# Token blocks of 512 in place of 448, 128 rows in a product of 113, and a subtraction moved to the head of its step: agent attention with two expert layers on one core

## The chip, the core and the metric

The kernel runs on one core of one Trainium2 chip. The core's engines run beside each other, each in the order of its own queue, and wait for each other by semaphores: TensorE (PE, matrix products and transposes into PSUM), VectorE (DVE), ScalarE (ACT), GpSimd (POOL, here only constants and some loads) and SyncE (SP, which issues DMAs). Before a matmul its stationary operand, the weights, is loaded by an instruction of its own (PEld in the profile); the other operand moves through the array column by column. The metric is device time in microseconds (us), the median of several executions; lower is better.

## What is computed

12480 tokens of 128 channels go through an attention with 49 agents and then two layers of width 2048 with squared ReLU, all in float32:

```python
def sm(a, b):                                   # softmax of scaled scores
    s = scale * (a @ b.transpose(0, 2, 1))
    e = np.exp(s - s.max(-1, keepdims=True))
    return e / (e.sum(-1, keepdims=True) + 1e-09)
agent_v = sm(agents, k) @ v
x = sm(q, agents) @ agent_v                     # 12480 x 128
g = s * np.maximum(x @ w_in, 0)**2 + b          # first layer
x = g @ w_out
h = np.maximum(x @ w_in2, 0)                    # second layer
out = (h * h) @ w_out2
```

## The kernel before

**Numbers in two parts.** Nearly all products run on numbers of 32 bits that TensorE takes rounded. To keep precision each operand is split into a high part (rounded) and a low part (the rest): `split` casts and then subtracts. A product of two such operands is three matmuls: low weights by high data, high by low, high by high.

**Preparation.** The attention of the agents over the keys gives a 49 x 128 matrix (`av`). `m_piece` multiplies it with `w_in`, so that the first layer's up product can go straight from the query softmax: `M`, high and low, holds `agent_v @ w_in` on partitions 0 to 48 and again on 64 to 112. The softmax of a block's queries stands in `X` with its high part in one of these places and its low part in the other, the gap between being zero. One product over 113 partitions (`KS` = 64 + 49) then sums both parts. Weights are decoded into their two parts on DVE and ACT by `fill`, in small steps that go on into the first 22 steps of the main loop.

**The main loop.** `blocks` cuts the tokens into 27 blocks of 448 (4 x 112) and one of 384. Each block takes 8 steps (`NPR`), and a step handles 2 of the 16 chunks of the width 2048. In a step PE does, in this order: `up1` of block t (four matmuls, 113 rows, low and high part of M), one query task of block t+1, `up2` of an earlier block (six), and the two `down` products of earlier steps (six each). Layer 2 runs 11 steps behind layer 1, and a down product 2 steps behind its up product. After an up product ACT applies ReLU and square, and DVE casts (`gh`) and subtracts (`gl`).

**Query tasks of block t+1 during block t.** Loading: two or three blocks ahead, on SP. `q_transpose` casts the high part `qh` (ACT, last step of the block before). `q_low` subtracts the low part `ql` (DVE) in step 0, behind `up1`'s cast and subtraction in DVE's queue. Step 1: `q_scores_T`, two matmuls with the stacked agents `aS` as weights (line 213). Step 2: `q_back`, a pair of transposes (line 228). Then softmax on ACT and DVE, and in step 6 `q_stack`, another pair of transposes (line 259), from which `X` of the next block is written.

The order of all engines is that of the code; nothing reorders it. The queue of each engine is filled step by step as the loop writes it. Line 594 is `up1`'s matmul, 604 `up2`'s, 620 both downs', 213 the score matmuls', 186 `q_low`'s subtraction, 124 and 125 the cast and subtraction of `split`.

Of the kernel before, what the change touches and what calls it, by code (L numbers as in the profile page):

```python
# [9 lines left out]
F32 = mybir.dt.float32  # L10
F32R = mybir.dt.float32r
# [3 lines left out]
ALU = mybir.AluOpType  # L15
AX = mybir.AxisListType

P = 128
BP = 112
SQ = 32  # L20
LAG = 2
WC = 512
# [11 lines left out]
DIRECT = 3  # L34
# [11 lines left out]
def tile_agent_attention_two_moe(  # L46
# [14 lines left out]
    nc = tc.nc  # L61
    _, N, C = q.shape
    NA = agents.shape[1]
# [7 lines left out]
    def cut(rows, most=P):  # L71

        pieces, t = [], 0
        while N - t >= rows * most:
            pieces.append((t, most, rows))
            t += rows * most
        if t < N:
            left = N - t
            p = next(x for x in range(min(most, left), 0, -1) if left % x == 0 and left // x <= rows)
            pieces.append((t, p, left // p))  # L80
        return pieces

    blocks = cut(4, BP)
    kblocks = cut(8)
    NT = sum(j for _, _, j in kblocks)

# [19 lines left out]
    aT = const.tile([P, GAP], F32, name="aT")  # L106
    s_sb = const.tile([P, 1], F32, name="s_sb")
    M = [const.tile([P, DFF], F32R, name=f"M{x}") for x in "hl"]
    av = [const.tile([P, KS], F32R, name=f"av{x}") for x in "hl"]
    b_sb = const.tile([P, 1], F32, name="b_sb")  # L110
    ones_r = const.tile([P, P], F32R, name="ones_r")
    y1_bias = const.tile([P, 1], F32, name="y1_bias")
    wo = [const.tile([P, NCH, C], F32R, name=f"wo{x}") for x in "hl"]
    wi2 = [const.tile([P, DFF], F32R, name=f"wi2{x}") for x in "hl"]
    wo2 = [const.tile([P, NCH, C], F32R, name=f"wo2{x}") for x in "hl"]
    stacks = [const.tile([P, 4, GAP], F32, name=f"stack{i}") for i in range(2)]
    sTs = [const.tile([KS, 256], F32, name=f"sT{i}") for i in range(2)]
    aS = const.tile([P, KS], F32R, name="aS")
    halves = (0, slice(0, NA)), (1, slice(GAP, KS))
    Xs = [const.tile([KS, 512], F32R, name=f"X{i}") for i in range(2)]  # L120

    def split(dst, src, eng_lo, copy=nc.vector.tensor_copy):

        copy(dst[0], src)  # L124
        eng_lo.tensor_tensor(out=dst[1], in0=src, in1=dst[0].bitcast(F32), op=ALU.subtract)  # L125
# [80 lines left out]
    def q_scores_T(t):  # L206

        _, p, j = blocks[t]
        n = p * j
        x = qT.pop(t)  # L210
        ps = small("ps_sT")
        for z in (1, 0):
            nc.tensor.matmul(out=ps[:KS, :n], lhsT=aS, rhs=x[z][:, :n], start=(z == 1), stop=(z == 0))  # L213
        sT = sTs[t % 2]
        for h, to in halves:
            nc.scalar.copy(sT[to, :2 * p], ps[:NA, 2 * p * h:2 * p * (h + 1)])
        for h, to in halves:
            nc.vector.tensor_tensor(
                out=sT[to, :2 * p], in0=ps[GAP:KS, 2 * p * h:2 * p * (h + 1)], in1=sT[to, :2 * p], op=ALU.add
            )  # L220
        q_sT[t] = sT
# [157 lines left out]
    def m_piece(i):  # L379

        sl = slice(i * WC, (i + 1) * WC)
        ps = small("ps_M")
        for z, (x, w) in enumerate(((av[0], wi[1]), (av[1], wi[0]), (av[0], wi[0]))):
            nc.tensor.matmul(out=ps[:KS], lhsT=x, rhs=w[:, sl], start=(z == 0), stop=(z == 2))
        split((M[0][:KS, sl], M[1][:KS, sl]), ps[:KS], nc.vector, nc.scalar.copy)

    with tc.manual_schedule():

        with tc.tile_pool(name="pre", bufs=1) as pre, tc.tile_pool(name="kp", bufs=2) as kp:
# [43 lines left out]
            nc.tensor.transpose(out=ps[:, :NA], in_=ag, identity=ident[:NA, :NA])  # L433
            nc.vector.tensor_copy(aT[:, :NA], ps[:, :NA])
            nc.vector.tensor_copy(aS[:, :NA], aT[:, :NA])
            nc.vector.tensor_tensor(out=aS[:, GAP:], in0=aT[:, :NA], in1=aS[:, :NA].bitcast(F32), op=ALU.subtract)
            mxa = pre.tile([P, 8, NA], F32, name="mxa")

            def k_transpose(g):
# [148 lines left out]
        def up1(t, i):  # L588
            n = blocks[t][1] * blocks[t][2]
            ps = ps_h.tile([P, 2, 512], F32, tag="h", name="ps_h1")  # L590
            for c in range(2):
                sl = slice((2 * i + c) * P, (2 * i + c + 1) * P)
                for z in (1, 0):
                    nc.tensor.matmul(out=ps[:, c, :n], lhsT=M[z][:KS, sl], rhs=X[t], start=(z == 1), stop=(z == 0))  # L594
            G1[t, i] = hidden(ps, n, 1, nc.scalar.copy if t * NPR + i in HI_ACT else nc.vector.tensor_copy)

        def up2(t, i):
# [48 lines left out]
        for st in range(total + L2 + LAG + 1):  # L646
# [10 lines left out]
                m_piece(2 + M_AT.index(st))  # L657
            if st < len(FILL_L):
                fill(FILL_L[st])
            if t < NB:  # L660
                up1(t, i)
                if i == 0:
                    for u, far in ((t + 2, t + 2 < DIRECT), (t + 3, DIRECT <= t + 3 < NB)):
                        if far:
                            q_load(u)
                if t + 1 < NB:
                    if t + 2 < NB and i == NPR - 2:
                        q_turn(t + 2)
                    elif t + 2 < NB and i == NPR - 1:
                        q_transpose(t + 2)  # L670
                    elif i == 0 and t + 1 >= DIRECT:
                        q_low(t + 1)
                    if i == QS[0]:
                        (q_scores if t + 1 < DIRECT else q_scores_T)(t + 1)
                    elif i == QS[1] and t + 1 >= DIRECT:
                        q_back(t + 1)
                    elif i == QS[3]:
                        q_norm(t + 1)
                    elif i == QS[4]:
                        q_stack(t + 1)  # L680
# [43 lines left out]
```

## Time and profile before

| | us |
|---|---|
| median of 3 runs | 1110.24 (1109.37 to 1111.34) |
| profiled execution, its own time | 1110.83 |
| its span, first to last instruction | 1108.9 |
| PE busy | 1092.6 |
| weight loads busy | 1009.6 |
| DVE busy | 954.7 |
| ACT busy | 952.8 |
| mean granted TensorE clock | 0.993 |

Busy times overlap. The end of a matmul is modelled and matmuls are pipelined: a 448-column matmul shows 0.36 us while the next one starts 0.20 us after it. So a matmul's cost is read from the starts. In the rows below a line of the timeline gives start (us), duration (us), engine, line, operation, output <- operands, shapes; text in brackets is the time the engine sat idle before it and what ended that.

### The profile page before, as it was taken

The numbers are of one execution on the slowest core, as the hardware profiler recorded it, in microseconds if no ns is written. First come the engines' busy times: TensorE is split into PE (matmuls) and PEld (weight loads), VectorE is DVE, ScalarE is ACT, GpSimd is POOL, SyncE is SP. The second block draws the span as 40 slices with busy tenths as digits, with TensorE's granted clock in tenths as the row PEclk, the third lists the DMA queues.
The fourth block names the chain that finished last, engine by engine and source line by source line (L and its number), as shares of the span: only waits on it lengthen the run. The fifth ranks groups of instructions, "written<-read, shape, count | busy, mean of one in ns | idle before, by whom it ended". The sixth has DMA issues, their size and how long they took to land.

```text
span 1108.9 us, 15258 instructions
## 1 busy us (share of the span) xinstructions
PE 1092.6 (99%) x5651; PEld 1009.6 (91%) x5651; DVE 954.7 (86%) x1413; ACT 952.8 (86%) x1201; POOL 12.5 (1%) x36
## 2 busy tenths in 40 slices
PE   9988999999999999999999999999999999999998
PEld 8877899999999999999999999999999999999997
DVE  6898888888888888888888888888888888888876
ACT  6658988988898889888888888888888888889876
POOL 2100000000000000000000000000000000000000
PEclk9898999999999999999999999999999999999999
DMA  9999939964999909999099991899963999700001
GB/s 343 291 162 15 8 11 10 14 19 12 15 8 15 21 9 8 15 15 19 5 15 15 15 8 17 13 15 7 15 19 12 9 14 15 12 9 1 9 9 16
DMA packets 1163202, 34.95 MB, mean 32 GB/s; under 512 B 1145575, under 2 KB 1159544, under 8 KB 1163128
## 3 DMA queue, kind: packets, MB, share of 16 engines
q1 hardware_dynamic: 1160224, 27.57, 103.5%
q0 software_dynamic: 1728, 6.29, 1.9%
q8 instruction: 44, 0.72, 0.4%
q14 instruction: 30, 0.25, 0.1%
q10 hardware_dynamic: 1176, 0.12, 0.1%
HBM read 27.58 MB, written 6.39 MB: 31 GB/s over the span
## 4 chain that ended last, share of the span: by engine, by line
PE 89%; DVE 3%; ACT 1%; DMA 1%; issue 1%; DVEq 0%; ACTq 0%
PE ps_y L620 47%; PE ps_h L604 24%; PE ps_h L594 16%; PE ps_sT L213 1%; DMA raw<-in_moe_w_out_dram 1%; DVE gl L125 1%; ACT r L583 1%; ACT r L584 1%; PE ps_x L259 0%; PE ps_b L228 0%; DVE gh L124 0%; DVE z L312 0%; DVE x L307 0%; DVE S L522 0%; DVE ex L315 0%
## 5 line engine op out<-in xcount | busy, mean ns | idle before, releaser
L125 DVE TENSOR_TENSOR gl<-r,gh 128x896 fp32r<-128x896 f32 (+2 forms) x450 | 487.6, 1083 | 17.3 <-ACT gh L124 2.0
L583 ACT ACTIVATE r<-ps_h 128x896 f32<-128x896 f32 (+2 forms) x450 | 408.8, 908 | 82.3 <-PE ps_h L594 62.1
L584 ACT ACTIVATE r<-r 128x896 f32<-128x896 f32 (+2 forms) x450 | 426.7, 948 | 14.3
L124 DVE CAST gh<-r 128x896 fp32r<-128x896 f32 (+2 forms) x445 | 275.2, 618 | 109.5 <-ACT r L584 106.2
L604 PE MATMUL ps_h<-yh,wi2l 128*128 128x448 f32 (+1 forms) x448 | 168.1, 375 | 0.3 <-ACT r L583 0.3
L594 PE MATMUL ps_h<-X,Ml 113*128 113x448 f32 (+1 forms) x448 | 165.2, 369 | 2.5 <-DVE X L270 1.3
L594 PE MATMUL ps_h<-X,Mh 113*128 113x448 f32 (+1 forms) x448 | 164.2, 366 | 0.0
L620 PE MATMUL ps_y<-gh,wol 128*128 128x448 f32 (+1 forms) x448 | 162.8, 363 | 1.0 <-ACT y L628 1.0
L604 PE MATMUL ps_h<-yh,wi2h 128*128 128x448 f32 (+1 forms) x448 | 163.4, 365 | 0.0
L620 PE MATMUL ps_y<-gl,woh 128*128 128x448 f32 (+1 forms) x448 | 162.5, 363 | 0.6 <-DVE gl L125 0.6
L604 PE MATMUL ps_h<-yl,wi2h 128*128 128x448 f32 (+1 forms) x448 | 163.0, 364 | 0.0
L620 PE MATMUL ps_y<-gh,woh 128*128 128x448 f32 (+1 forms) x448 | 162.4, 363 | 0.0
L620 PE MATMUL ps_y<-gl,wo2h 128*128 128x448 f32 (+1 forms) x448 | 162.2, 362 | 0.1
L620 PE MATMUL ps_y<-gh,wo2l 128*128 128x448 f32 (+1 forms) x448 | 162.0, 362 | 0.0
L620 PE MATMUL ps_y<-gh,wo2h 128*128 128x448 f32 (+1 forms) x448 | 162.0, 362 | 0.0
L594 PEld LDWEIGHTS ps_h<-X,Ml 113*128 113x128 f32 x448 | 84.7, 189 | 9.5 <-issue 3.3
L620 PEld LDWEIGHTS ps_y<-gh,wol 128*128 128x128 f32 x448 | 84.5, 189 | 7.6 <-ACT y L628 1.4
L594 PEld LDWEIGHTS ps_h<-X,Mh 113*128 113x128 f32 x448 | 85.4, 191 | 6.5
L604 PEld LDWEIGHTS ps_h<-yh,wi2l 128*128 128x128 f32 x448 | 84.1, 188 | 7.1 <-ACT r L583 0.7
L604 PEld LDWEIGHTS ps_h<-yl,wi2h 128*128 128x128 f32 x448 | 84.6, 189 | 6.4
L620 PEld LDWEIGHTS ps_y<-gl,woh 128*128 128x128 f32 x448 | 84.4, 188 | 6.6 <-DVE gl L125 0.9
L604 PEld LDWEIGHTS ps_h<-yh,wi2h 128*128 128x128 f32 x448 | 84.0, 187 | 7.0
(122 smaller groups left out, 942.9 us busy)
## 6 DMA issues: line engine op xcount, KB each, us to landing
kraw<-in_k_dram SPq DMA_DIRECT2D x12, 512.0 KB, 10.9
v<-in_v_dram SPq DMA_DIRECT2D x12, 512.0 KB, 8.3
out_dram<-o SPq DMA_DIRECT2D x108, 56.0 KB, 1.9
q_raw<-in_q_dram SPq DMA_DIRECT2D x21, 224.0 KB, 36.3
raw<-in_moe_w_out_dram POOLq DMA_DIRECT2D x8, 512.0 KB, 7.9
raw<-in_moe_w_in_dram SPq DMA_DIRECT2D x4, 512.0 KB, 7.8
raw<-in_moe_w_in_dram POOLq DMA_DIRECT2D x4, 512.0 KB, 7.6
q_raw<-in_q_dram SPq DMA_DIRECT2D x24, 56.0 KB, 2.2
```

Of the source, the lines that this page charges most:

```text
L124: copy(dst[0], src)
L125: eng_lo.tensor_tensor(out=dst[1], in0=src, in1=dst[0].bitcast(F32), op=ALU.subtract)
L213: nc.tensor.matmul(out=ps[:KS, :n], lhsT=aS, rhs=x[z][:, :n], start=(z == 1), stop=(z == 0))
L583: nc.scalar.activation(r[:, c, :n], ps[:, c, :n], AF.Relu)
L584: nc.scalar.activation(r[:, c, :n], r[:, c, :n], AF.Square)
L594: nc.tensor.matmul(out=ps[:, c, :n], lhsT=M[z][:KS, sl], rhs=X[t], start=(z == 1), stop=(z == 0))
L604: nc.tensor.matmul(out=ps[:, c, :n], lhsT=w[:, sl], rhs=y[:, :n], start=(z == 0), stop=(z == 2))
L620: nc.tensor.matmul(out=py[t][:, :n], lhsT=wz[:, m], rhs=g[:, c, :n], start=(m == 0 and z == 0), stop=(m == NCH - 1 and z == 2),)
```

## The change

Three things, and what they need:

- The main loop's blocks become 23 of 512 tokens (4 x 128), one of 384 and one of 320: 25 in all. The preparation's blocks stay.
- `av` and `aS` are 128 columns wide in place of 113, filled up with zeros; `m_piece` writes all 128 rows of `M`, and `X` has 128 rows, of which the last fifteen are zero. The first up product runs over 128 rows, and the score matmuls have 128 weight columns.
- `q_low` is issued at the head of step 0, ahead of `up1`.

The resident tiles are listed in another order, with an unused tile of 104 numbers ahead of `X`.

```diff
-BP = 112
+TAIL = [96, 80]
...
-    blocks = cut(4, BP)
+    blocks, left = [], N
+    for p in [P] * (N // (4 * P) - 1) + TAIL:
+        blocks.append((N - left, p, 4))
+        left -= 4 * p
...
-    aS = const.tile([P, KS], F32R, name="aS")
+    aS = const.tile([P, P], F32R, name="aS")
+    av = [const.tile([P, P], F32R, name=f"av{x}") for x in "hl"]
...
+    const.tile([P, 104], F32, name="apart")
+    Xs = [const.tile([P, 512], F32R, name=f"X{i}") for i in range(2)]
...
-            nc.tensor.matmul(out=ps[:KS, :n], lhsT=aS, rhs=x[z][:, :n], start=(z == 1), stop=(z == 0))
+            nc.tensor.matmul(out=ps[:, :n], lhsT=aS, rhs=x[z][:, :n], start=(z == 1), stop=(z == 0))
...
-            nc.tensor.matmul(out=ps[:KS], lhsT=x, rhs=w[:, sl], start=(z == 0), stop=(z == 2))
-        split((M[0][:KS, sl], M[1][:KS, sl]), ps[:KS], nc.vector, nc.scalar.copy)
+            nc.tensor.matmul(out=ps, lhsT=x, rhs=w[:, sl], start=(z == 0), stop=(z == 2))
+        split((M[0][:, sl], M[1][:, sl]), ps, nc.vector, nc.scalar.copy)
...
-                    nc.tensor.matmul(out=ps[:, c, :n], lhsT=M[z][:KS, sl], rhs=X[t], start=(z == 1), stop=(z == 0))
+                    nc.tensor.matmul(out=ps[:, c, :n], lhsT=M[z][:, sl], rhs=X[t], start=(z == 1), stop=(z == 0))
...
+            if i == 0 and DIRECT <= t + 1 < NB:
+                q_low(t + 1)
             if t < NB:
                 up1(t, i)
...
-                    elif i == 0 and t + 1 >= DIRECT:
-                        q_low(t + 1)
```

On DVE, at the seam of two blocks (gh1 and gl1 are the parts of a first-layer hidden pair, gh2 and gl2 of a second-layer one, ql and qh the parts of the queries), the program before has:

```order
L124 CAST gh2_1704<-r_1703 128x2x448
L125 TENSOR_TENSOR gl2_1705<-r_1703,gh2_1704 128x2x448
L124 CAST gh1_1728<-r_1727 128x2x448
L125 TENSOR_TENSOR gl1_1729<-r_1727,gh1_1728 128x2x448
L186 TENSOR_TENSOR ql_1694<-qt_1646,qh_1693 128x448
L124 CAST gh2_1745<-r_1744 128x2x448
L125 TENSOR_TENSOR gl2_1746<-r_1744,gh2_1745 128x2x448
```

and the changed program:

```order
L129 CAST gh2_1705<-r_1704 128x1024
L130 TENSOR_TENSOR gl2_1706<-r_1704,gh2_1705 128x1024
L191 TENSOR_TENSOR ql_1695<-qt_1647,qh_1694 128x512
L129 CAST gh1_1730<-r_1729 128x1024
L130 TENSOR_TENSOR gl1_1731<-r_1729,gh1_1730 128x1024
L129 CAST gh2_1746<-r_1745 128x1024
L130 TENSOR_TENSOR gl2_1747<-r_1745,gh2_1746 128x1024
```

The subtraction of ql has moved ahead of one hidden pair of the first layer; the hidden pair is one stretch of 1024 in place of two of 448.

On PE, in step 1 of a block, around the score matmuls, the program before has:

```order
L594 MATMUL ps_h1_1410<-X0_91,Mh_73 128x448
L213 MATMUL ps_sT_1422<-ql_1341,aS_90 113x448
L213 MATMUL ps_sT_1422<-qh_1340,aS_90 113x448
L604 MATMUL ps_h2_1429<-yh_1151,wi2l_83 128x448
L604 MATMUL ps_h2_1429<-yl_1152,wi2h_82 128x448
```

and the changed program:

```order
L599 MATMUL ps_h1_1411<-X0_91,Mh_73 128x512
L218 MATMUL ps_sT_1423<-ql_1342,aS_85 128x512
L218 MATMUL ps_sT_1423<-qh_1341,aS_85 128x512
L609 MATMUL ps_h2_1430<-yh_1152,wi2l_78 128x512
L609 MATMUL ps_h2_1430<-yl_1153,wi2h_77 128x512
```

PE's order is the same within a step; the sizes are what differs, and the number of blocks.

## Rows read from the trace of the kernel before

**Rows 1.** The page's first part: busy us (share of the span) and instructions.

```profile
PE 1092.6 (99%) x5651; PEld 1009.6 (91%) x5651; DVE 954.7 (86%) x1413; ACT 952.8 (86%) x1201; POOL 12.5 (1%) x36
```

**Rows 2.** Timeline of PE, a plain step: first up, first down, next step.

```profile
599.16 0.37 PE L594 MATMUL ps_h<-X,Ml 113*128 113x448 f32 x1
...
601.21 0.36 PE L620 MATMUL ps_y<-gh,wol 128*128 128x448 f32 x1
...
603.61 0.37 PE L594 MATMUL ps_h<-X,Ml 113*128 113x448 f32 x1
```

**Rows 3.** The same view, the step with the scores, and the next block's scores.

```profile
608.05 0.37 PE L594 MATMUL ps_h<-X,Ml 113*128 113x448 f32 x1
...
608.67 0.36 PE L594 MATMUL ps_h<-X,Mh 113*128 113x448 f32 x1
608.92 0.46 PE L213 MATMUL ps_sT<-ql,aS 128*113 128x448 f32 x1
609.22 0.36 PE L213 MATMUL ps_sT<-qh,aS 128*113 128x448 f32 x1
...
613.04 0.37 PE L594 MATMUL ps_h<-X,Ml 113*128 113x448 f32 x1
...
645.42 0.46 PE L213 MATMUL ps_sT<-ql,aS 128*113 128x448 f32 x1
```

**Rows 4.** The same view, the step with a pair of transposes, and the next step's start.

```profile
613.86 0.35 PE L228 MATMUL ps_b<-ident,sT 113*112 113x113 f32 x2
613.98 0.45 PE L604 MATMUL ps_h<-yh,wi2l 128*128 128x448 f32 x1
...
617.68 0.37 PE L594 MATMUL ps_h<-X,Ml 113*128 113x448 f32 x1
```

**Rows 5.** Busy us by stretch: length, PE, PEld, DVE, ACT, POOL (instructions), clock, DMA, GB/s.

```profile
83.00:90.00 7.00, 6.97 (x20) 6.05 (x21) 5.53 (x9) 4.81 (x7) 0.00 (x0) 0.54 1.87 9
600.00:636.50 36.50, 36.50 (x184) 33.70 (x183) 32.29 (x47) 32.45 (x40) 0.00 (x0) 1.00 1.53 14
```

**Rows 6.** Timeline of PE near the end: 384-column matmuls, and up2 without up1.

```profile
1062.57 0.34 PE L594 MATMUL ps_h<-X,Ml 113*128 113x384 f32 x1
...
1063.28 0.37 PE L604 MATMUL ps_h<-yh,wi2l 128*128 128x448 f32 x1
...
1075.03 0.36 PE L604 MATMUL ps_h<-yh,wi2l 128*128 128x448 f32 x1
...
1076.23 0.34 PE L620 MATMUL ps_y<-gh,wol 128*128 128x384 f32 x1
...
1077.27 0.36 PE L620 MATMUL ps_y<-gh,wo2l 128*128 128x448 f32 x1
```

**Rows 7.** Timeline of PE in the preparation: 512-column matmuls, the last eight starts.

```profile
71.25 0.40 PE L506 MATMUL ps_cs<-wol,ones_r 128*128 128x512 f32 x1
...
73.11 0.39 PE L384 MATMUL ps_M<-Mh,avh 128*113 128x512 f32 x1
```

**Rows 8.** Timeline of DVE in step 0, ahead of the scores of rows 3.

```profile
606.57 0.63 DVE L124 CAST gh<-r 128x896 fp32r<-128x896 f32 x1 [0.39 <-ACT r L584]
...
608.24 0.62 DVE L186 TENSOR_TENSOR ql<-qt,qh 128x448 fp32r<-128x448 f32 x1
```

**Rows 9.** Waits of the weight loads, whole run: us in total, times, longest us.

```profile
PEld ps_sT L213 <- DVE ql L186: 6.5, 25, 0.3
```

**Rows 10.** Groups by shape, 200 to 1080 us: busy us, mean ns, idle before.

```profile
L125 DVE TENSOR_TENSOR gl<-r,gh 128x896 fp32r<-128x896 f32 x380 | 415.1, 1092 | 13.1
L584 ACT ACTIVATE r<-r 128x896 f32<-128x896 f32 x379 | 362.2, 956 | 12.0
...
L125 DVE TENSOR_TENSOR gl<-r,gh 128x768 fp32r<-128x768 f32 x8 | 7.7, 958 | 0.3
L584 ACT ACTIVATE r<-r 128x768 f32<-128x768 f32 x8 | 6.8, 846 | 0.3
```

**Rows 11.** Timeline of PE, downs after an early pair of transposes, and the next step.

```profile
140.71 0.37 PE L620 MATMUL ps_y<-gh,wol 128*128 128x448 f32 x1
...
143.19 0.37 PE L594 MATMUL ps_h<-X,Ml 113*128 113x448 f32 x1
```

More of the change, by code (lines that the diff above doesn't have):

```diff
@@ L81, in cut @@
         return pieces
-    blocks = cut(4, BP)
+    blocks, left = [], N
+    for p in [P] * (N // (4 * P) - 1) + TAIL:
+        blocks.append((N - left, p, 4))
+        left -= 4 * p
+    assert left == 0 and all(4 * p % (2 * SQ) == 0 for p in TAIL)
     kblocks = cut(8)
@@ L108, in tile_agent_attention_two_moe @@
     M = [const.tile([P, DFF], F32R, name=f"M{x}") for x in "hl"]
[L109 to L112, printed above, removed]
     wo = [const.tile([P, NCH, C], F32R, name=f"wo{x}") for x in "hl"]
@@ L117, in tile_agent_attention_two_moe @@
     sTs = [const.tile([KS, 256], F32, name=f"sT{i}") for i in range(2)]
-    aS = const.tile([P, KS], F32R, name="aS")
+    aS = const.tile([P, P], F32R, name="aS")
+    av = [const.tile([P, P], F32R, name=f"av{x}") for x in "hl"]
+    b_sb = const.tile([P, 1], F32, name="b_sb")
+    y1_bias = const.tile([P, 1], F32, name="y1_bias")
+    const.tile([P, 104], F32, name="apart")
+    Xs = [const.tile([P, 512], F32R, name=f"X{i}") for i in range(2)]
+    ones_r = const.tile([P, P], F32R, name="ones_r")
     halves = (0, slice(0, NA)), (1, slice(GAP, KS))
-    Xs = [const.tile([KS, 512], F32R, name=f"X{i}") for i in range(2)]
     def split(dst, src, eng_lo, copy=nc.vector.tensor_copy):
@@ L435, in tile_agent_attention_two_moe @@
             nc.vector.tensor_copy(aS[:, :NA], aT[:, :NA])
-            nc.vector.tensor_tensor(out=aS[:, GAP:], in0=aT[:, :NA], in1=aS[:, :NA].bitcast(F32), op=ALU.subtract)
+            nc.vector.tensor_tensor(out=aS[:, GAP:KS], in0=aT[:, :NA], in1=aS[:, :NA].bitcast(F32), op=ALU.subtract)
             mxa = pre.tile([P, 8, NA], F32, name="mxa")
```

## The prediction

> **What bounds the kernel now.** I read the page first: TensorE (PE) is busy 99% of the span, VectorE (DVE) and ScalarE (ACT) 86% each [rows 1]. A busy PE is not yet a PE at its peak, so the next view is PE's timeline in the middle of the run, where the distance from one matmul's start to the next one's start says what each really costs. In a plain step (four matmuls of the first up product, six of the second, twelve of the two down products) the twelve downs take from 601.21 to 603.61, 2.40 us, so 0.200 each; the ten ups before them take 599.16 to 601.21, 2.05 us, 0.05 more than ten times 0.200 [rows 2]. 448 columns at one column per cycle of 2.4 GHz are 0.1867, so a matmul costs its columns and about 0.0133 that doesn't look like columns. The blocks of 384 at the end say the same: six downs from 1076.23 to 1077.27, 1.04 us, 0.1733 each, which is 0.160 and again 0.0133 [rows 6]. So the price is 0.0133 + columns/2400 us, and every matmul carries the fixed part.
>
> The main loop repeats exactly: the query scores of one block start at 608.92 and of the next at 645.42, 36.50 us [rows 3]. 176 main matmuls at 0.200 are 35.20 of that. The other 1.30 I lay out by steps. A plain step is 599.16 to 603.61, 4.45 us, 0.05 over 22 x 0.200 [rows 2]. The step with the scores is 608.05 to 613.04, 4.99 us [rows 3]: the pair of score matmuls at 0.200 is 0.40, the plain 0.05 is in it too, and 0.14 is left. That 0.14 is a wait: the last matmul of the first up product stands at 608.67 and the next starts 0.25 later instead of 0.20, and the second score matmul starts 0.30 after the first [rows 3], and the weight loads of this line waited for the low part of the queries (ql) 25 times, 6.5 us in all [rows 9]. The step with a pair of transposes is 613.04 to 617.68, 4.64 us, 0.24 over 4.40 [rows 4]; the other such step is the same length. About 0.02 of it is the first up product's own share, so a pair of transposes costs 0.22. Left over from 36.50: 35.20 + 0.40 + 0.14 + 0.44 leaves 0.32 per block.
>
> I put that 0.32 to the 113-row matmuls of the first up product. The spacing is off only from its first matmul on, and through the six matmuls behind it, and then returns to 0.200. Where the first up product has ended, the same six of the second up product run from 1075.03 to 1076.23, 1.20 us, 0.200 each [rows 6]. Its weights and its 448 columns are the same as in [rows 2]; only the 113-row matmuls ahead of it are gone. DVE and ACT have 4 us of slack in a block (32.29 and 32.45 busy of 36.50 [rows 5]), so PE sets the pace and every 0.0133 counts.
>
> **The change part by part.**
>
> *Blocks of 512.* 28 blocks become 25 for the same 12480 tokens. The columns stay; the fixed 0.0133 goes for 3 x 178 matmuls: 534 x 0.0133 = **7.1 us**. This needs that 512 columns cost 0.2267. The trace has few such matmuls, and they speak against it: the last eight of the preparation take 71.25 to 73.11, 1.86 us, 0.2325 each [rows 7]. But they are a short run right after a stall, of two kinds of weights, some 113 columns wide, and the main loop too needs a few matmuls after a stall to come back to its spacing. I take the line through 384 and 448, which are long, undisturbed runs of the same code, and keep 0.2325 as a rival. Three blocks fewer also save three times two pairs of transposes, 3 x 0.44 = 1.3; the transposes' weights grow from 112 to 128 columns, which costs nothing at least and, in proportion to the two that take 0.12 us until the next start, 0.02 per block at most, 0.4 in all: **0.9 us**.
>
> The Trainium skill (TensorE: Matmul & The Clock Gate, section "Back-to-back issue gap") gives columns/2.4 + 2.5 ns for a matmul at full clock. By it the fixed part would be 0.0025 and the first term 1.3 us in place of 7.1; the spacing of 0.200 [rows 2] differs, and the measurement decides.
>
> *DVE and ACT at 512.* The low-part subtraction goes from 958 to 1092 ns between 768 and 896 elements, the square from 846 to 956 [rows 10], so at 1024 about 1226 and 1066: 12% more per block, where PE's block grows from 36.50 to 176 x 0.2267 + 2 x 0.2267 + 0.46 = 40.81, also 12%. Their slack stays at 11%; cost nothing. If that cover failed, PE would wait for PSUM, which no row of the main loop shows.
>
> *128 rows in the first up product.* The fifteen added rows hold zeros; no instruction is added, the weights stay 128 columns and the moving columns are the same. If the odd row count is what disturbs the spacing, 0.32 per block goes. I count 26 blocks of the 28, since early in the loop PE waits for other engines anyway: **8.3 us**. The bounds are nothing (the disturbance stays) and this.
>
> *The low part of the queries at the head of a step.* On DVE one subtraction of 0.62 us moves ahead of the cast and subtraction of the first hidden pair: from 608.24 to before 606.57, where DVE has 0.39 idle [rows 8]. It then ends about 607.2 at the latest, 1.4 us before PE asks for it at 608.67. Its own input, the rounded queries, is copied by ACT a step earlier. Behind it in DVE's queue stand the cast and subtraction of that hidden pair, some 0.3 later than now; their first reader is the down product two steps on, some 9 us. It issues no DMA and passes no queue but DVE's; the query loads stay where they are on SP. So the wait of 0.14 goes 25 times: **3.5 us**. Late next would be the transposed scores, which end behind DVE's next pair and scale with the block as PE does. If DVE were still behind, up to 3.5 comes back.
>
> *Order of the resident tiles, wider aS and av.* Zeros more to write at the start by GpSimd; nothing.
>
> Sum: 7.1 + 0.9 + 8.3 + 3.5 = 19.8 us. The profiled execution took 1110.83 us (span 1108.9), 0.6 over the median of 1110.24. 1110.83 - 19.8 = 1091.0; against the median **1090.4 us**.
>
> What I can't work out is the start of the main loop: there PE also waits for DVE and ACT, which still decode weights, and from 83 to 90 us the granted clock is at a mean of 0.54, almost all of it at the lower level of 1.2 GHz (20 matmuls in 6.97 us [rows 5], which at 0.200 would be 4.0). Wider blocks put more PE work and more DVE work into those steps alike. If that stretch shifts or goes, up to 3 us either way. So the forecast's own range is 1087 to 1094.
>
> **The rivals.**
>
> *The 113 rows are not the cause* and the disturbance stays (15%). For it: nothing in the matmul needs fewer cycles with more rows, and the change leaves X and M as they lie. Against it: the six undisturbed matmuls of [rows 6]. The disturbance shrinks with narrower blocks: 1062.57 to 1063.28, four matmuls of 384 columns in 0.71 us, 0.02 over 4 x 0.1733 [rows 6]. So per block it would be 0.32 if it stays and up to 0.48 at 512 if it grows on: 23 x 0.32 to 0.48 = 7.4 to 11, or **1098 to 1101.5 us**. The Trainium skill (the same page, section "LDWEIGHTS (loading the stationary operand)") has this rule: loading weights depends on the columns, and the number of rows doesn't matter. By that rule this rival is what happens; [rows 2, 6] lean the other way without settling it, since they take the whole product away and not its row count.
>
> *PE falls into a longer spacing and nothing resets it* (slower, 15%). The trace has a second steady spacing: after a small wait at a pair of transposes the downs run from 140.71 to 143.19, twelve in 2.48 us, 0.2067 each, until the next 113-row matmuls come [rows 11]; then 0.200 returns. With 128 rows everywhere there is no such matmul. If the main loop at 512 stays at 0.0067 more, or at the 0.2325 of [rows 7] (0.0058 more), 23 blocks x 178 matmuls cost 24 to 27 us: 1090.4 + 24 to 27 = **1114 to 1118 us**, slower than before. It decides from 19.8 / 4094 = 0.0048 on, that is at 0.2315 per matmul. Against it: in the main loop both pairs of transposes of every block come back to 0.200 each time, and every block repeats the last.
>
> *The longer spacing holds for a part of a block* (15%): entered at one pair of transposes and left at the other, four of eight steps, 4 x 22 x 0.0067 x 23 = 13.5: **1104 us**.
>
> *ql is still late* (5%): **1094 us**.
>
> **How the numbers follow.** Forecast 50%, rows 15%, part of a block 15%, whole block 15%, ql 5%. Ends of 1086 (the start gains a little more than counted) and 1105 leave out the whole-block rival and little else. A measurement of this kernel tells 0.2%, 2.2 us, from no change. Below 1108: the forecast, ql, rows and part of a block, less some spread, 0.82. Within: 0.04. Above 1112.5: 0.14.
>
> **What would show it.** In the profile after: downs 0.227 apart; the ten ups of a plain step 2.27 and not 2.32 or more; a plain step 4.99; score matmuls 0.227 apart with no weight load waiting for ql; block period 40.8. Downs at 0.231 or more make the prediction wrong by themselves; ups with excess behind X show that the rows were not it.

## The result

The changed kernel is slower: 1118.85 us (1117.53 to 1121.42, four runs) against 1110.72 us (1109.37 to 1111.34) for the kernel before on the same chip, a ratio of 1.0078 with an interval of 1.0066 to 1.0091. The forecast was 1090.4 us, with a range of 1086 to 1105. The profiled execution of the changed kernel took 1117.77 us, its span is 1115.8 us and its mean granted clock 0.995.

The lines of the page that answer to [rows 1]; busy us (share of the span) and instructions:

```profile
span 1115.8 us, 13795 instructions
PE 1099.6 (99%) x5105; PEld 904.5 (81%) x5105; DVE 935.2 (84%) x1278; ACT 929.9 (83%) x1081; POOL 12.5 (1%) x36
```

TensorE still sets the pace, and DVE and ACT still have slack. The windows view, one block of the main loop (us, then busy us and instructions of each engine; the column behind POOL is the granted clock), answers to [rows 5]:

```profile
600.00:642.05 42.05, 42.05 (x184) 33.87 (x183) 35.47 (x46) 35.97 (x41) 0.00 (x0) 1.00 0.42 9
```

PE is busy throughout, at a granted clock of 1.00, and DVE and ACT are idle for 6 to 6.6 of the 42.05 us: the cover that the prediction named held. What costs is the matmuls themselves. PE's timeline of the changed kernel, a step with a score pair and the starts of two blocks (start, duration, line, operation, output <- operands, shapes; lines are 5 higher than before: 599 is the first up product, 609 the second, 625 the downs, 218 the scores):

```profile
601.40 0.40 PE L599 MATMUL ps_h<-X,Ml 128*128 128x512 f32 x1
...
602.34 0.39 PE L218 MATMUL ps_sT<-ql,aS 128*128 128x512 f32 x1
602.56 0.40 PE L218 MATMUL ps_sT<-qh,aS 128*128 128x512 f32 x1
602.80 0.39 PE L609 MATMUL ps_h<-yh,wi2l 128*128 128x512 f32 x1
...
604.20 0.40 PE L625 MATMUL ps_y<-gh,wol 128*128 128x512 f32 x1
...
607.01 0.40 PE L599 MATMUL ps_h<-X,Ml 128*128 128x512 f32 x1
...
644.38 0.39 PE L218 MATMUL ps_sT<-ql,aS 128*128 128x512 f32 x1
```

The scores of two blocks stand 644.38 - 602.34 = 42.04 us apart; the forecast was 40.81. Twelve downs take 607.01 - 604.20 = 2.81 us, 0.2342 each and not 0.2267. The four ups take 602.34 - 601.40 = 0.94 us, 0.235 each, so they have no excess of their own. The second score matmul starts 0.22 after the first where it was 0.30 [rows 3], and the next matmul 0.24 later. In the view of waits of the weight loads (us in total, times, longest), where ql stood first with 6.5 us in [rows 9], it doesn't come up any more; the first row is now

```profile
PEld ps_h L599 <- issue: 2.8, 2, 1.6
```

So the wait that the prediction wanted gone is gone.

At the end, where the blocks of 384 and 320 run, the spacing is as short as it can be (the same view):

```profile
1086.10 0.34 PE L609 MATMUL ps_h<-yh,wi2l 128*128 128x384 f32 x1
...
1087.14 0.31 PE L625 MATMUL ps_y<-gh,wol 128*128 128x320 f32 x1
...
1088.02 0.34 PE L625 MATMUL ps_y<-gh,wo2l 128*128 128x384 f32 x1
```

Six of 384 columns take 1.04 us, 0.1733 each as in [rows 6]; six of 320 take 0.88, 0.1467 each, again 0.0133 over the columns. So of the widths in this kernel it is 512 alone that is long. 42.04 - 40.81 = 1.23 us per block, times 23 blocks, is 28.3 us: 1090.4 + 28.3 = 1118.7, which is the measured time to within 0.2. No second effect of any size is needed. The question is why 512 columns cost 0.234.

### The profile page after: what moved, and what is told of

It reads as the page before. It is cut to its first block, busy times and chain, and to the rows that moved or that the text cites. A ratio compares the mean times of both kernels' runs of the same rounds, so it can differ in the third digit from the quotient of the medians.

```text
span 1115.8 us, 13795 instructions
## 1 busy us (share of the span) xinstructions
PE 1099.6 (99%) x5105; PEld 904.5 (81%) x5105; DVE 935.2 (84%) x1278; ACT 929.9 (83%) x1081; POOL 12.5 (1%) x36
## 4 chain that ended last, share of the span: by engine, by line
PE 93%; DMA 3%; ACT 1%; DVE 1%; issue 1%; SPq 0%; DVEq 0%
PE ps_y L625 48%; PE ps_h L609 25%; PE ps_h L599 16%; PE ps_av L544 2%; DMA kraw<-in_k_dram 2%; DMA q_raw<-in_q_dram 1%; PE ps_sT L218 1%; ACT r L588 0%; PE ps_x L264 0%; ACT r L589 0%; PE ps_b L233 0%; DVE gl L130 0%; PE ps_cs L511 0%; PE ps_M L389 0%; DVE gh L129 0%
## 5 line engine op out<-in xcount | busy, mean ns | idle before, releaser
L588 ACT ACTIVATE r<-ps_h 128x1024 f32<-128x1024 f32 (+3 forms) x402 | 399.9, 995 | 117.0 <-PE ps_h L599 109.2
L130 DVE TENSOR_TENSOR gl<-r,gh 128x1024 fp32r<-128x1024 f32 (+3 forms) x402 | 479.8, 1194 | 15.9 <-ACT gh L129 2.3
L589 ACT ACTIVATE r<-r 128x1024 f32<-128x1024 f32 (+3 forms) x402 | 416.5, 1036 | 12.8
L129 DVE CAST gh<-r 128x1024 fp32r<-128x1024 f32 (+2 forms) x397 | 267.6, 674 | 138.1 <-ACT r L589 131.7
L609 PE MATMUL ps_h<-yh,wi2l 128*128 128x512 f32 (+2 forms) x400 | 159.2, 398 | 0.0
L599 PE MATMUL ps_h<-X,Ml 128*128 128x512 f32 (+2 forms) x400 | 156.4, 391 | 2.0 <-DVE X L275 1.2
L625 PE MATMUL ps_y<-gh,wol 128*128 128x512 f32 (+2 forms) x400 | 157.1, 393 | 0.9 <-ACT y L633 0.9
L625 PE MATMUL ps_y<-gl,wo2h 128*128 128x512 f32 (+2 forms) x400 | 156.7, 392 | 0.1
L625 PE MATMUL ps_y<-gh,wo2l 128*128 128x512 f32 (+2 forms) x400 | 156.5, 391 | 0.0
L625 PE MATMUL ps_y<-gh,woh 128*128 128x512 f32 (+2 forms) x400 | 156.4, 391 | 0.0
```

Source lines behind the costliest of these rows:

```text
L588: nc.scalar.activation(r[:, c, :n], ps[:, c, :n], AF.Relu)
L589: nc.scalar.activation(r[:, c, :n], r[:, c, :n], AF.Square)
L599: nc.tensor.matmul(out=ps[:, c, :n], lhsT=M[z][:, sl], rhs=X[t], start=(z == 1), stop=(z == 0))
L609: nc.tensor.matmul(out=ps[:, c, :n], lhsT=w[:, sl], rhs=y[:, :n], start=(z == 0), stop=(z == 2))
L625: nc.tensor.matmul(out=py[t][:, :n], lhsT=wz[:, m], rhs=g[:, c, :n], start=(m == 0 and z == 0), stop=(m == NCH - 1 and z == 2),)
```

## Experiments

Each kernel was timed beside the kernel before on the same chip; the ratio is to that kernel. Not all rows are from one chip, so across rows the ratios are safer than the times.

| kernel | us | ratio and interval |
|---|---|---|
| e1, after with blocks of 448 | 1102.74 | 0.9918 (0.9901 to 0.9936) |
| e2, after with 113 rows | 1118.04 | one run, no interval |
| e3, after with blocks of 480 | 1112.87 | 1.0016 (1.0006 to 1.0027) |
| e4, after with the distance of operands 0 | 1092.05 | 0.9823 (0.9807 to 0.9839) |
| e5, e1 with X at distance 160 | 1099.92 | 0.9897 (0.9882 to 0.9912) |
| e6, before with X at distance 160 | 1113.54 | 1.0021 (1.0011 to 1.0030) |
| e7, before with q_low at the head | 1106.62 | 0.9966 (0.9956 to 0.9977) |
| e8, e1 with q_low back | 1109.67 | 0.9983 (0.9972 to 0.9994) |
| e9, e3 with distance 128 | 1120.05 | 1.0083 (1.0055 to 1.0111) |
| e10, after with distance 192 | 1114.00 | 1.0029 (1.0017 to 1.0042) |
| e11, e4 with all moved 96 bytes | 1090.77 | 0.9826 (0.9811 to 0.9840) |
| e12, after with all moved 96 bytes | 1117.25 | 1.0059 (1.0042 to 1.0076) |

### Width, rows or place: the first four kernels

**e1: the other two parts without the wide blocks.**

```diff
-    for p in [P] * (N // (4 * P) - 1) + TAIL:
+    for p in [112] * 27 + [96]:
```

> The changed kernel with its blocks back at 27 of 448 and one of 384; 128 rows, wide aS and av, the early low part and the new order of tiles stay. Theory W (a matmul of 512 columns costs more than its columns and the fixed 0.0133 us, through its width alone): downs at 0.2000, ups without excess, no wait for ql, block period 36.50 - 0.32 - 0.14 = 36.04, so 1110.7 - 8.3 - 3.5 = about 1099 us. Theory R (with 128 rows everywhere nothing brings PE back from the longer spacing): downs at 0.2067, 28 x 176 x 0.0067 = 33 us more than that, about 1130 us. Theory P (the new places of the tiles slow PE down): spacing off 0.2000 here too.

Measured: 1102.74 us. PE's timeline of e1, a step with the scores:

```profile
603.87 0.37 PE L599 MATMUL ps_h<-X,Ml 128*128 128x448 f32 x1
...
604.48 0.37 PE L599 MATMUL ps_h<-X,Mh 128*128 128x448 f32 x1
604.68 0.37 PE L218 MATMUL ps_sT<-ql,aS 128*128 128x448 f32 x1
604.89 0.37 PE L218 MATMUL ps_sT<-qh,aS 128*128 128x448 f32 x1
...
605.30 0.37 PE L609 MATMUL ps_h<-yl,wi2h 128*128 128x448 f32 x1
```

The wait for ql is gone (0.20 and 0.21 where it was 0.25 and 0.30). The excess behind X is smaller but not gone: 605.30 - 603.87 = 1.43 for seven matmuls, 0.03 over 1.40. So those two parts gain 8.6 us (against 1111.34 on its chip), and the wide blocks lose some 16.

**e2: the rows alone.** At 512, does a matmul of 113 rows bring the short spacing back?

```diff
-                    nc.tensor.matmul(out=ps[:, c, :n], lhsT=M[z][:, sl], rhs=X[t], start=(z == 1), stop=(z == 0))
+                    nc.tensor.matmul(out=ps[:, c, :n], lhsT=M[z][:KS, sl], rhs=X[t][:KS], start=(z == 1), stop=(z == 0))
```

> The changed kernel with the first up product on 113 rows again, blocks of 512 kept. Theory W: downs at about 0.234 as in the changed kernel, the ups the same or worse, 1118 to 1125 us. Theory R: the 113-row matmuls bring PE back each step, downs at 0.2267, 23 x 96 x 0.0073 = 16 us less, about 1103 us.

Measured: 1118.04 us, a block of 42.03 us. The ten ups of a plain step of e2:

```profile
612.84 0.39 PE L599 MATMUL ps_h<-X,Ml 113*128 113x512 f32 x1
...
615.17 0.39 PE L625 MATMUL ps_y<-gh,wol 128*128 128x512 f32 x1
```

They take 2.33 us, 0.233 each, and the downs stay at 0.234; nothing changes. The prediction's rival "nothing resets it" had nearly the right size and the wrong mechanism.

**e3: a width between** (the last block's output is cut at 256).

```diff
-    for p in [P] * (N // (4 * P) - 1) + TAIL:
+    for p in [120] * 26:
...
-            cuts = (0, n) if t < NB - 1 else (0, n // 2, n)
+            cuts = (0, n) if t < NB - 1 else (0, 256, n)
```

> The changed kernel with 26 blocks of 480 tokens. Theory W with the threshold above 480: spacing 0.2133, two fixed parts fewer than with 448 (2 x 178 x 0.0133 = 4.7 us), about 1094 us. Theory W with a cost that grows from 448 on: spacing 0.217 to 0.220, 26 x 178 x 0.0035 to 0.0067 = 16 to 31 us more, 1110 to 1125 us. Theory R: 0.220, about 1125 us.

Measured: 1112.87 us. Six of the second up product in e3:

```profile
606.59 0.38 PE L609 MATMUL ps_h<-yh,wi2l 128*128 128x480 f32 x1
...
607.90 0.38 PE L625 MATMUL ps_y<-gh,wol 128*128 128x480 f32 x1
```

They take 1.31 us, 0.218 each; the downs of the main loop have a mean of 0.217. Columns and 0.0133 would be 0.2133. So 480 columns are long too, by half of what 512 are.

**m1: streams of one kind of matmul.** Ahead of the main loop, 48 matmuls in a row of each kind (110 of the mixed one), with nothing to wait for. Only the matmul is shown.

```diff
...
+                    nc.tensor.matmul(
+                        out=ps[:wcols, :N], lhsT=wo[0 if same else n % 2][:r, 0 if same else n % NCH, :wcols],
+                        rhs=M[n // 2 % 2][:r, off:off + N], start=(n == 0), stop=(n == count - 1),
+                    )
...
```

> The changed kernel with streams of 48 matmuls put ahead of the main loop, results unused: widths 320, 384, 448, 464, 480, 496, 504, 508, 512; then 512 with the moving operand 4, 8, 16, 32, 64, 128 numbers further; 512 with one weight tile only; 448 again; 448 with 113 rows; 448 with 4 of 22 matmuls on 113 rows; 512 with 113 rows; 512 and 448 with 113 weight columns; 448. About 220 us longer. Theory W: the spacing leaves columns/2400 + 0.0133 at one width between 448 and 512 and is about 0.234 at 512 for every offset. Theory P: it changes with the offset. Theory R: 448 and 512 alike are off by 0.0067 behind a disturbance and come back with 113 rows. 448 with 4 of 22 on 113 rows should show 0.05 per 22 if the row count disturbs the main loop.

Measured, the settled spacing in ns (here and in m2 and m3 the mean of a stream's last 16 spacings): 512 columns at 226.7 (as forecast), with 113 rows 226.7, with 113 weight columns 226.7. But with the moving operand 16 bytes further on 231.7, 32 bytes 233.4, 64 bytes 228.9, 128 bytes 232.3, and at 256 and 512 bytes 226.7 again. So a 512-column matmul can cost 0.2267: the width alone isn't it, and neither are rows. For 448 columns m1 has 202.7 with 128 rows (206.7 in the first of three such streams), 202.7 with 113, and 203.1 over the whole stream with four of 22 on 113 rows: in a stream the row count doesn't cost the 0.05 per 22 that the main loop of the kernel before had.

What counts is where the operands lie, modulo 256 bytes. By the addresses of the built programs, in this kernel and the one before, all weights of the main loop's products lie at 160 modulo 256, X and qh at 128, and the hidden parts, y and ql at 64. So X and qh lie 224 bytes behind their weights modulo 256, and the others 160; M and wo, the operands of the streams, lie at a distance of 0.

### Place: the distance of the two operands

**m2: the same streams over all places**, 32 matmuls each, with M moved in steps of 16 or 32 bytes over the weights `wo`.

```diff
...
+            for N_ in (512, 448):
+                for off in range(0, 68, 4):
+                    stream(N_, off)
+            for N_ in (480, 384):
+                for off in range(0, 64, 8):
+                    stream(N_, off)
```

> The changed kernel with streams of 32 matmuls ahead of the main loop, results unused, weights and moving operand with fixed tiles: width 512 and then 448 with the moving operand 0, 16, 32, ... 256 bytes further; 480 and 384 at 0, 32, ... 224 bytes; then 512 and 448 each at 0, 160, 0, 32, 0, 160, 4, 8 bytes. About 330 us longer. Theory A (the spacing hangs on the distance of the two operands' places, modulo 256 bytes, together with the width): the same spacing comes back at 0 and 256 and each time an offset is repeated; 512 at 160 about 0.234 and at 0 0.2267; 448 at 160 0.2000 and at 0 more. Theory H (it hangs on what ran before): repeats of an offset differ.

Settled spacing in ns, by the distance in bytes (columns / 2400 plus 13.3 would be 173.3, 200.0, 213.3 and 226.7):

| columns | 0 | 32 | 64 | 96 | 128 | 160 | 192 | 224 |
|---|---|---|---|---|---|---|---|---|
| 384 | 173.3 | 173.4 | 173.3 | 176.6 | 175.9 | 173.4 | 174.9 | 173.4 |
| 448 | 202.4 | 204.5 | 200.1 | 205.4 | 203.9 | 200.0 | 202.5 | 204.5 |
| 480 | 216.7 | 220.0 | 218.3 | 220.0 | 213.4 | 217.6 | 215.9 | 220.0 |
| 512 | 226.7 | 233.3 | 228.7 | 233.2 | 233.3 | 234.3 | 233.4 | 233.3 |

At 160, where nearly all operands of this kernel lie, 448 columns are at their best and 512 are at the worst of the table. X lies at 224, where 448 columns have 204.5; that fits the excess behind X in e1, and e5 below tests it. PE's timeline of m2, the first matmul of streams of 512 columns at the distances 0, 160 and 0 again, 32 matmuls apart:

```profile
411.36 0.39 PE L579 MATMUL ps_t<-Mh,woh 128*128 128x512 f32 x1
...
418.61 0.40 PE L579 MATMUL ps_t<-Mh,woh 128*128 128x512 f32 x1
...
426.10 0.39 PE L579 MATMUL ps_t<-Mh,woh 128*128 128x512 f32 x1
```

32 take 7.25 us at distance 0 (0.2266 each) and 7.49 at 160 (0.2341 each). Of 512 columns every repeat of a distance comes back to within 0.1 ns. Of 448 columns one doesn't: at 32 bytes the first stream settles at 204.5 and the repeat at 206.7, with the same operands in the same places and no other engine busy. Only what ran before differs, so there Theory H has its part.

**e4: the changed kernel with the distance 0.** Room that nothing uses, 8 numbers more ahead of X and 12 more in each of two small tiles behind it, moves X and qh on by 32 bytes and the hidden parts, y and ql by 96.

```diff
-    const.tile([P, 104], F32, name="apart")
+    const.tile([P, 112], F32, name="apart")
...
-        sm = qp.tile([P, 4, 1], F32, tag="sm", name="sm")
+        sm = qp.tile([P, 16, 1], F32, tag="sm", name="sm")[:, :4]
```

> The changed kernel, with some 100 bytes of unused space put in so that X, the query parts, y and the hidden pairs lie at a distance from their weights that is 0 modulo 256 bytes (before and in the changed kernel: 160, and 224 for X). Theory A: downs and ups at 0.2267, block period 40.8, about 1118.9 - 23 x (42.05 - 40.8) = 1090 us, what was forecast. Theory W or H: no change, 1117 to 1121 us.

Measured: 1092.05 us, 1.8% faster than the kernel before and 2.4% faster than the changed one, with the same instructions. PE's timeline of e4, a plain step:

```profile
608.82 0.39 PE L599 MATMUL ps_h<-X,Ml 128*128 128x512 f32 x1
...
609.72 0.39 PE L609 MATMUL ps_h<-yh,wi2l 128*128 128x512 f32 x1
...
611.08 0.39 PE L625 MATMUL ps_y<-gh,wol 128*128 128x512 f32 x1
...
613.80 0.39 PE L599 MATMUL ps_h<-X,Ml 128*128 128x512 f32 x1
```

Ten ups take 2.26 us and twelve downs 2.72, 0.2267 each; the step is 4.98 (forecast 4.99) and the block 40.83 to 40.86 (forecast 40.81).

**e10: the control**, the first of the two edits alone. X and qh lie at 0, the rest at 192.

```diff
-    const.tile([P, 104], F32, name="apart")
+    const.tile([P, 112], F32, name="apart")
```

> The control of e4_512_0: the changed kernel with only its first bit of space put in, so that all the same tiles move, but the hidden pairs and y end at a distance of 192 in place of 0; X is at 0. Theory A: 192 of 512 columns ran at 0.2333 in m2_places, so downs at 0.233 and 1110 to 1118 us. If it were enough that the tiles move or that the space behind X is larger: 1092 us.

Measured: 1114.00 us. PE's timeline of e10:

```profile
612.24 0.39 PE L625 MATMUL ps_y<-gh,wol 128*128 128x512 f32 x1
...
615.04 0.39 PE L599 MATMUL ps_h<-X,Ml 128*128 128x512 f32 x1
```

Twelve downs take 2.80 us, 0.2333 each, as the streams at 192 do. It is not the moving of tiles that helps but where they come to lie.

**m3, e11 and e12: distance, or place of the moving operand?** So far the weights lay at the same place, 160 modulo 256, in every kernel, so both rules fitted. In m3 both operands of the streams move. e11 and e12 are e4 and the changed kernel with one more unused tile ahead of all weights:

```diff
+    const.tile([P, 24], F32, name="ahead")
     M = [const.tile([P, DFF], F32R, name=f"M{x}") for x in "hl"]
```

and m3's streams are those of m2 with

```diff
...
+                    at = n % (NCH - 1) * C + w
+                    nc.tensor.matmul(
+                        out=ps[:, :N], lhsT=wo[n % 2].rearrange("p a b -> p (a b)")[:, at:at + C],
+                        rhs=M[n // 2 % 2][:, off:off + N], start=(n == 0), stop=(n == count - 1),
+                    )
...
```

> After with streams of 32 matmuls ahead of the main loop (their results are used by nothing), 25 of 512 columns and 15 of 448, in which both operands move: the weights by 0, 32, 96, 160 or 224 bytes, the moving operand by 0, 32, 96, 160 or 224. In every kernel so far the weights lay at 160 modulo 256, so a rule on the distance of the two and a rule on the place of the moving operand alone gave the same. Theory D (distance): 512 runs at 0.2267 where both are moved alike, and at 0.231 to 0.2345 elsewhere, whatever the weights' place; 448 at 0.2000 where the moving operand is 160 ahead modulo 256, and between 0.2025 and 0.2067 elsewhere. Theory P (place of the moving operand): the columns of the table are alike: 512 at 0.2267 wherever the moving operand is moved by 0, whatever the weights do.

> The kernel with distance 0 and blocks of 512 (1092.05 us), with all resident tiles moved on by 96 bytes, so that weights and moving operands all lie at 0 modulo 256 in place of 160. Theory D (distance): nothing changes, 1091 to 1093, 0.2267 per matmul. Theory P (place of the moving operand): the moving operands lie 96 bytes on, where streams of 512 took 0.2311: 0.2311 - 0.2267 = 0.0044, times 4094, 18 us more: 1110.

> After with all resident tiles moved on by 96 bytes: the hidden parts, the queries and y come to lie at 160 modulo 256, where the moving operands of the fast version lie, and the weights at 0; the distances stay as in after. Theory D (distance): as after, 1117 to 1121, 0.234 per matmul. Theory P (place): the downs and second ups run at 0.2267, and with them nearly all of the gain of the fast version comes: 1092 to 1098.

Measured: 1090.77 us for e11 and 1117.25 for e12. PE's timeline of e11, then of e12 (their lines are one higher than those of the changed kernel):

```profile
607.56 0.39 PE L600 MATMUL ps_h<-X,Ml 128*128 128x512 f32 x1
...
609.83 0.39 PE L626 MATMUL ps_y<-gh,wol 128*128 128x512 f32 x1
```

```profile
609.00 0.40 PE L626 MATMUL ps_y<-gh,wol 128*128 128x512 f32 x1
...
611.81 0.40 PE L600 MATMUL ps_h<-X,Ml 128*128 128x512 f32 x1
```

Ten ups of e11 take 2.27 us, 0.227 each, and its downs run 0.2267 apart; twelve downs of e12 take 2.81, 0.234 each. Weights and hidden parts changed their places, and the time followed the distance. In m3 all five streams of 512 columns with both operands moved alike settle at 226.6 to 226.7, at five different places, and the twenty others at 228.7 to 234.3. The four that follow another stream need five to ten matmuls to get there. PE's timeline of m3, streams with weights and moving operand at (0, 160), then (32, 32) bytes, each with the stream behind it:

```profile
96.86 0.39 PE L580 MATMUL ps_t<-Mh,woh 128*128 128x512 f32 x1
...
104.35 0.40 PE L580 MATMUL ps_t<-Mh,woh 128*128 128x512 f32 x1
...
119.28 0.39 PE L580 MATMUL ps_t<-Mh,woh 128*128 128x512 f32 x1
...
126.56 0.40 PE L580 MATMUL ps_t<-Mh,woh 128*128 128x512 f32 x1
```

32 matmuls take 7.49 us and 7.28. For 448 columns the expectation of theory D holds only in part: two streams at the same distance 160 differ. PE's timeline, weights and moving operand at (0, 160), then (96, 0):

```profile
279.49 0.36 PE L580 MATMUL ps_t<-Mh,woh 128*128 128x448 f32 x1
...
285.90 0.37 PE L580 MATMUL ps_t<-Mh,woh 128*128 128x448 f32 x1
...
292.40 0.37 PE L580 MATMUL ps_t<-Mh,woh 128*128 128x448 f32 x1
...
299.01 0.36 PE L580 MATMUL ps_t<-Mh,woh 128*128 128x448 f32 x1
```

The first 32 take 6.41 us (0.2003), the second 6.61 (0.2066). So at 448 columns one distance has two steady spacings, and they are the two of the kernel before, 0.200 and the 0.2067 of [rows 11].

**e9: another width with its best place.** e3 with the operands at 128, where streams of 480 columns ran at 0.2133.

```diff
-    const.tile([P, 104], F32, name="apart")
+    const.tile([P, 144], F32, name="apart")
...
-        sm = qp.tile([P, 4, 1], F32, tag="sm", name="sm")
+        sm = qp.tile([P, 16, 1], F32, tag="sm", name="sm")[:, :4]
```

> The kernel of e3_480 with every moving operand at a distance of 128 modulo 256 bytes from its weights, where the streams of m2_places ran 480 columns at 0.2133. Theory A: spacing 0.2133 in the main loop, one block more than e4_512_0, 178 x 0.0133 = 2.4 us, so about 1094.5 us. If the streams don't carry over to the main loop: 1112.9 us as e3_480.

Measured: 1120.05 us, which neither expectation had. PE's timeline of e9:

```profile
607.17 0.38 PE L625 MATMUL ps_y<-gh,wol 128*128 128x480 f32 x1
...
609.81 0.38 PE L599 MATMUL ps_h<-X,Ml 128*128 128x480 f32 x1
```

Twelve downs take 2.64 us, 0.220 each (between 200 and 1000 us so do 109 of 162 such groups, and the other 53 take 2.61). The main loop settled on a longer spacing than the streams. Distance and width don't settle it alone: where there are two steady spacings, something decides which one is entered. What that is stays open.

### The other two parts, one at a time

**e7: q_low at the head, in the kernel before.**

```diff
+            if i == 0 and DIRECT <= t + 1 < NB:
+                q_low(t + 1)
...
-                    elif i == 0 and t + 1 >= DIRECT:
-                        q_low(t + 1)
```

> The kernel before with nothing but the low part of the queries at the head of its step. If the term of the forecast is right: no weight load waits for ql, score matmuls 0.205 or less apart, 25 x 0.14 = 3.5 us less, about 1107.5 us. If PE then waits elsewhere or falls into the longer spacing: no gain, 1110 us or more.

Measured: 1106.62 us against 1110.30, 3.7 us less. PE's timeline of e7, the scores of two blocks:

```profile
606.52 0.37 PE L213 MATMUL ps_sT<-ql,aS 128*113 128x448 f32 x1
...
642.88 0.37 PE L213 MATMUL ps_sT<-ql,aS 128*113 128x448 f32 x1
```

They stand 36.36 us apart; to the ns the blocks of the trace have 36.353 where they had 36.50, 0.147 less.

**e8: the rows alone**: e1 with the subtraction of ql back in its old place.

```diff
-            if i == 0 and DIRECT <= t + 1 < NB:
-                q_low(t + 1)
...
+                    elif i == 0 and t + 1 >= DIRECT:
+                        q_low(t + 1)
```

> The kernel of e1_448 (blocks of 448, 128 rows) with the low part of the queries back behind the first hidden pair. The wait of 0.14 per block is back: 1102.7 + 3.5 = about 1106 us; with e7_qlow it tells whether the two parts add up. If 128 rows took the wait away by themselves: 1102.7.

Measured: 1109.67 us, 0.6 less than the kernel before and not the 5 of e1 less e7. PE's timeline of e8:

```profile
609.32 0.36 PE L599 MATMUL ps_h<-X,Mh 128*128 128x448 f32 x1
609.59 0.47 PE L218 MATMUL ps_sT<-ql,aS 128*128 128x448 f32 x1
609.89 0.37 PE L218 MATMUL ps_sT<-qh,aS 128*128 128x448 f32 x1
```

The wait is a little longer (0.27 where it was 0.25), and blocks of 36.36 us, with the wait alone, are followed by blocks of 36.49 and 36.61, in which some of the groups of twelve downs run 0.2067 apart (24 of 176 groups between 200 and 1000 us, and none of 175 in the kernel before). So with 128 rows and the wait left in, PE is at times in the longer spacing, for a part of a block, as the prediction's third rival had it. That the wait puts it there is likely, since none of 177 groups of e1 has it, but what else it takes no run shows.

**e5 and e6: X at 160**, in e1 and in the kernel before:

```diff
-    const.tile([P, 104], F32, name="apart")
+    const.tile([P, 88], F32, name="apart")
     Xs = [const.tile([P, 512], F32R, name=f"X{i}") for i in range(2)]
+    const.tile([P, 16], F32, name="apart2")
```

```diff
+    const.tile([P, 48], F32, name="apart")
     Xs = [const.tile([KS, 512], F32R, name=f"X{i}") for i in range(2)]
+    const.tile([P, 16], F32, name="apart2")
```

> The kernel of e1_448 with X moved by 64 bytes, so that its distance from M is 160 modulo 256 like that of the other operands. Theory A: the last 0.02 of a step behind X goes, ups at 0.2000, 27 x 8 x 0.02 = 4 us less, about 1098.5 us. Theory H: no change, 1102.7 us.

> The kernel before with X moved by 192 bytes and all behind it by 256, so that X's distance from M is 160 modulo 256; still 113 rows. Theory A alone: the ten ups of a plain step take 2.00 and not 2.05, 8 us less, about 1102.5 us. If the row count is a cause of its own: some of the 0.05 stays, 1104 to 1111 us.

Measured: e5 1099.92 us, e6 1113.54. PE's timeline of e5, a plain step:

```profile
612.15 0.36 PE L600 MATMUL ps_h<-X,Ml 128*128 128x448 f32 x1
...
612.95 0.36 PE L610 MATMUL ps_h<-yh,wi2l 128*128 128x448 f32 x1
...
614.15 0.36 PE L626 MATMUL ps_y<-gh,wol 128*128 128x448 f32 x1
...
616.55 0.36 PE L600 MATMUL ps_h<-X,Ml 128*128 128x448 f32 x1
```

All 22 are 0.200 apart, 4.40 in all, and a block is 36.05 us: 35.20 + 0.40 + 0.44 and no rest. The same view of e6, a plain step and then one with the scores:

```profile
605.23 0.36 PE L596 MATMUL ps_h<-X,Ml 113*128 113x448 f32 x1
...
607.27 0.36 PE L622 MATMUL ps_y<-gh,wol 128*128 128x448 f32 x1
...
609.67 0.36 PE L596 MATMUL ps_h<-X,Ml 113*128 113x448 f32 x1
...
612.26 0.37 PE L622 MATMUL ps_y<-gh,wol 128*128 128x448 f32 x1
...
614.75 0.37 PE L596 MATMUL ps_h<-X,Ml 113*128 113x448 f32 x1
```

In the plain step the ten ups take 2.04 us and the twelve downs 2.40: with 113 rows the excess behind X is still there (2.05 in 75 of 109 plain steps between 200 and 1000 us, 2.02 in 34, where e5 has 2.00 in all). In the step with the scores twelve downs take 2.49 us, 0.207 each; 39 of 174 groups are like that, and none of the kernel before. So with 113 rows and ql late the place of X gains nothing, and the block is 36.55 to 36.67. The expectation, 1102.5 to 1111, missed this. The same with ql early was not run.

## Why the prediction was wrong

**The step that failed** is the first term, 534 x 0.0133 = 7.1 us, and in it the sentence "This needs that 512 columns cost 0.2267". They cost 0.234, 1.23 us more per block, so the term is not a gain of 7.1 us but a loss of 21.2 (7.1 - 28.3). The price hangs on the distance of the operands as well as on the width, and the prediction had it as a matter of the width alone. With the operands at distance 0 the sum comes out: e4, the same program otherwise, takes 1092.05 us, 1.7 from the forecast. That this includes the whole term of the rows is in part luck, since e4 moves X too, which the prediction left where it was.

**Where it came from.** [rows 7] had 512-column matmuls at 0.2325, and the prediction set them aside for the line through 384 and 448 because those were "long, undisturbed runs". They were so for a reason that the line can't know: by m2 both widths are at their best at the distance 160, where most operands of this kernel lie. The change kept all distances and altered the width, and at 160 a width of 512 is at its worst. The edge that the prediction gave, 0.2315 per matmul, was passed by 0.003. That [rows 7] came so near the price of the main loop is partly luck. By the addresses of the built program `ones_r` and `wo` there are 32 bytes apart, where m2 has 233.3; but the pieces of M, six matmuls, are at a distance of 0, where m3 needs five to ten matmuls to settle at 226.7. For those the prediction's objection, a short run, was right.

**The rival that came true** was sized nearly right (1114 to 1118 us) and given 15%; its mechanism was not right. It said that a matmul of 113 rows resets the spacing; e2 puts that matmul back and changes nothing. Its argument against itself, that blocks return to 0.200 after each stall, was true of 448 columns and said nothing of 512, where a stream at the distance 160 is long each time, whatever ran before it (m2 and m3).

**Fewer blocks** (7.1 and 0.9 us): right, once the spacing is columns/2400 + 0.0133 at both widths. e5 and e4 differ by 1099.92 - 1092.05 = 7.9 us, forecast 8.0. The other price that the prediction weighed, columns/2.4 + 2.5 ns by the Trainium skill (TensorE: Matmul & The Clock Gate, section "Back-to-back issue gap"), would give 1.3 + 0.9; these two kernels speak for the 0.0133 of the rows.

**128 rows** (8.3 us): the size was nearly right for two causes together, the reason only half, and the rival "the 113 rows are not the cause" was half right. The 0.32 per block has 113 rows and X's place in it. From e7 to e1, 36.353 to 36.20, the rows take away 0.15 (with them come the 128 columns of `aS` and `av` and the new order of tiles, which were not tried alone); from e1 to e5, 36.20 to 36.05, the place takes away the other 0.15. Neither e6 (place without rows, the wait left in) nor e8 (rows with the wait left in) gains anything like its share, so the parts don't add up one by one. The change itself left X at 224. Why 113 rows cost in the main loop and not in the streams of m1 stays open.

The rule of the Trainium skill (TensorE: Matmul & The Clock Gate, section "LDWEIGHTS (loading the stationary operand)") that the time of a load hangs on the columns of the weights and not on their rows, agrees with the loads' own duration in the kernel before, 188 and 189 ns with 113 rows and 187 to 189 with 128. It is a rule for the load; the spacing in the main loop at 448 columns is another matter, and there 113 rows do cost: ten ups of a plain step take 2.05 us in e7 and 2.02 in e1.

**The wait for ql** (3.5 us): right, 3.7 in e7, and no wait took its place in the changed kernel. At 448 columns it costs more in the program with 128 rows than in the one with 113: 1109.67 - 1102.74 = 6.9 us from e1 to e8.

**DVE and ACT cost nothing; the start within 3 us:** right. From 135 to 1040 us the view of waits has no row of PE or of its weight loads in the changed kernel. The stretch of half clock, [rows 5], did not grow: from 83 to 90 us the granted clock has a mean of 0.76 where it was 0.54. The 0.9 for the transposes was not measured by itself; it is part of the 7.9 above.

## What to carry to other kernels

Where TensorE sets the pace, the price of a matmul is its spacing in the trace at just the width and the places of operands that the new kernel will have; a price extrapolated from other widths needs a stream of the new matmuls, some 32 long, measured first. Even that is no proof: at 480 columns the main loop of e9 ran at 0.220 where the stream had 0.2133. When tiles change their width or order, look at the distance of each moving operand from its weights modulo 256 bytes: a few unused numbers between the tiles were worth 2.4% here. Rows of the very shape that is to come, when they speak against a line drawn through others, want an explanation before they are set aside.

## What the runs showed of the hardware

A 512-column matmul of this rounded 32-bit type, with its weights loaded by an instruction of its own, follows the one before by 0.2267 us where moving operand and weights lie at the same place modulo 256 bytes (m1, m2, m3, e4, e11), or 240 bytes apart (226.7 in m2), and by 0.229 to 0.235 at the other multiples of 16 bytes; 4 bytes apart it is 0.237 (m2). The same distances order the widths 384, 448 and 480 in other ways, so none of the eight distances of the table is the best for all. At 448 and 480 columns a distance can have two steady spacings (448: 0.200 and 0.2066 at 160 in m3, 0.2045 and 0.2067 at 32 in m2; 480: 0.2133 in the stream and 0.220 in e9 at 128). For the pair of m2, whose operands are the same, what went before decides between them; for the others that is not shown.

The Trainium skill (SBUF — State Buffer, section "A bandwidth-pool intuition that's wrong (but worth ruling out)") gives TensorE a second, independent read port for loading weights. One could take from it that it does not matter to the moving operand where the weights lie; m3 (226.7 against 234.3 ns at 512 columns) and the kernels e4, e11 and e12 show that their distance does matter. What inside the chip makes the distance count, and how what went before chooses between two spacings, no run here shows.
